# A longer first chunk and two buffers for the first attention pairs, in front of a TensorE-bound feed-forward layer

## The chip, the cores and the metric

The kernel runs on one core of one Trainium2 chip. The metric is the device time of one execution in microseconds (us). Five instruction streams run side by side on a core, each in the order in which it was built: TensorE (PE, matmuls; its weight loads are PEld), VectorE (DVE), ScalarE (ACT), GpSimd (POOL) and SyncE (SP), which here issues every DMA. SBUF is the working memory, PSUM the memory that TensorE writes.

## What is computed

Attention over 8 batches, 8 heads, 576 positions of 64 numbers, and behind it a feed-forward layer over the 4608 rows that come out of it:

```python
q_d, k_d, v_d = (a.reshape(B, H, 144, 4, D).mean(axis=3) for a in (q, k, v))
out_up = np.repeat(softmax(scale * q_d @ k_d.T) @ v_d, 4, axis=2)          # pooled
scores = np.where(abs(i - j) < 4, scale * q @ k.T, -1e9)                   # local band
x = out_up + softmax(scores) @ v                                            # (4608, 512)
h = x @ w_in                                                                # d_ff = 2048
g = np.where(h >= 1, h, np.where(h <= -1, 0.0, (h + 1) ** 2 / 4))
out = g @ w_out
```

(The softmax subtracts the row's maximum and divides by the sum plus 1e-9.)

## The kernel before

A **pair** is two heads of one batch; there are 32, four to a batch, written a0 to a31. For a pair, the 576 positions are covered by ten windows of 64, so local scores are twenty 64x64 products (`sl_ps`, L168), to which DVE adds a band mask (L186). DVE takes the row maximum, POOL subtracts it (L194), ACT takes the exponential (L197), DVE sums and divides. The pooled scores go the same way in three blocks of 48 queries (`sp_ps`, L178), for which ACT first writes q, scaled, into a block-diagonal tile `q_bd` (L153), so that one product serves both heads on 96 rows; ACT also divides them (L222). TensorE transposes both (`tl_ps` L234, `tp_ps` L243), ACT copies them out, TensorE multiplies with v (`pl_ps` L262, `pp_ps` L274), and DVE and ACT and POOL add them up and split x into a high and a low part, `xh` and `xl` (L283 to L295), in a ring of 1152 columns: two batches.

The feed-forward layer runs over 12 **chunks** of 384 columns, three to the ring, and 16 blocks f of 128 hidden units. A **step** is one (chunk, f): twelve matmuls into `h_ps` (`mm1`, L405), the activation on ACT, DVE and ACT (L416 to L421) giving `gh`, the rest `gl` on POOL (L422), and nine matmuls with 512 columns into three `o_ps` (`mm2`, L443). Chunk 0 needs batch 0 alone, chunk 1 and 2 also batch 1.

Weights arrive as raw 64-bit words, and each of 32 half-megabyte tiles is **converted** (`convert_weights`, "c" in the tables): two passes on ACT (L319, L322), two on DVE (L323, L324), a cast on ACT (L326), a subtraction on POOL (L327).

The order of the start is written out by hand in `BEFORE_STEPS` and `FIRST_STEPS`: q3 loads q and k of a3, v loads v of a0, w loads two weight tiles, c converts one, a5 goes on with a5 to its next yield, s is the next `mm1`, m the next `mm2`. A scheduler then orders each engine's stream, with `mm1`'s activation at a higher priority. Chunks 0 and 2 are split: both run first over f 0 to 7, then chunk 1 over all, then the other half of chunks 0 and 2; half sums of chunks 0 and 2 go through DRAM (`partial`). a8 to a11 are in the table; later pairs come from `attn_step`, one over four steps, in two chunks of three. When `FIRST_STEPS` ends, `mm2` is two steps behind `mm1`, and the loop that follows keeps it so.

One buffer each holds q, k, vp (v for pooling), v, qd, kd, sp, al, ap; PSUM tiles rotate for a0 to a3 over two (`rot1`) and three (`rot2`) buffers, and are single later.

Of the kernel before, what the change touches and what calls it, by code (L numbers as in the profile page):

```python
# [99 lines left out]
def attention_then_ffn(ctx: ExitStack, tc, qT, kT, vw, vp, band, w_in, w_out, out):  # L100
# [40 lines left out]

    def attention(n, pool_1, pool_2):
# [3 lines left out]
        M = 2 * QB  # L146


        qd = apool.tile([P, SD], F32, name="qd", tag="qd", bufs=1)
        nc.vector.tensor_reduce(qd, q.rearrange("p (s f) -> p s f", f=FACTOR), axis=AX.X, op=ALU.add)  # L150
        for h in range(2):
            hs = slice(h * D, (h + 1) * D)
# [5 lines left out]
        kd = apool.tile([P, SD], F32, name="kd", tag="kd", bufs=1)  # L158
# [367 lines left out]
```

## Time and profile before

| | |
|---|---|
| three runs | 1003.66, 1007.73, 1008.30 us (median 1007.73) |
| the profiled execution | 1004.22 us, of it 1002.4 us from first to last instruction (the span) |
| PE busy | 964.6 us (96%) |
| ACT, POOL, DVE busy | 534.6, 389.5, 364.1 us |
| mean granted TensorE clock | 0.985 of full speed |
| the chain that ended last | PE 85% of the span; `h_ps` 38%, `o_ps` 37% |
| DMA | 69.37 MB |

The chain is followed back from the last instruction; where it names one engine all along, that engine's own instructions add up to the time. Matmuls overlap, so a single one's duration is longer than the distance between two starts, and it is the distance that counts.

### The profile page before, as it was taken

The numbers are of one execution on the slowest core, as the hardware profiler recorded it, in microseconds if no ns is written. First come the engines' busy times: TensorE is split into PE (matmuls) and PEld (weight loads), VectorE is DVE, ScalarE is ACT, GpSimd is POOL, SyncE is SP. The second block draws the span as 40 slices with busy tenths as digits, with TensorE's granted clock in tenths as the row PEclk, the third lists the DMA queues.
The fourth block names the chain that finished last, engine by engine and source line by source line (L and its number), as shares of the span: only waits on it lengthen the run. The fifth ranks groups of instructions, "written<-read, shape, count | busy, mean of one in ns | idle before, by whom it ended". The sixth has DMA issues, their size and how long they took to land.

```text
span 1002.4 us, 18310 instructions
## 1 busy us (share of the span) xinstructions
PE 964.6 (96%) x7412; PEld 852.2 (85%) x7412; DVE 364.1 (36%) x646; ACT 534.6 (53%) x1221; POOL 389.5 (39%) x359
## 2 busy tenths in 40 slices
PE   5598999999999999999999999999999999999998
PEld 4477788899888888998888888999888888999997
DVE  5766464312445441113444343113334443111111
ACT  5768587544565555335555555434555555433433
POOL 3756664422345433223333344222344434222222
PEclk8699999999999999999999999999999999999999
DMA  7876210001324211002221222000212310000000
GB/s 261 297 263 229 79 52 33 0 1 56 113 75 137 74 50 57 1 1 80 63 62 50 81 61 62 32 1 26 80 52 73 97 58 14 33 1 1 32 1 31
DMA packets 28260, 69.37 MB, mean 69 GB/s; under 512 B 3344, under 2 KB 3344, under 8 KB 28176
## 3 DMA queue, kind: packets, MB, share of 16 engines
q1 hardware_dynamic: 28176, 68.20, 21.0%
q8 instruction: 58, 0.95, 0.4%
q14 instruction: 26, 0.21, 0.1%
...
## 4 chain that ended last, share of the span: by engine, by line
PE 85%; ACT 1%; DVE 1%; POOL 1%; issue 0%; DVEq 0%; ACTq 0%; POOLq 0%
PE h_ps L405 38%; PE o_ps L443 37%; PE sp_ps L178 2%; PE sl_ps L168 2%; PE pl_ps L262 2%; PE pp_ps L274 2%; PE tp_ps L243 1%; PE tl_ps L234 1%; POOL xl L295 0%; POOL sl L194 0%; POOL gl L422 0%; ACT u L417 0%; ACT u L416 0%; DVE sp_ps L212 0%; ACT gh L421 0%
## 5 line engine op out<-in xcount | busy, mean ns | idle before, releaser
L405 PE MATMUL h_ps<-xh,w_i 128*128 128x384 f32 x1536 | 404.3, 343 | 1.7 <-DVE u L418 1.4
L422 POOL TENSOR_TENSOR gl<-u,gh 128x384 fp32r<-128x384 f32 x192 | 195.4, 1018 | 505.6 <-ACT gh L421 391.0
L443 PE MATMUL o_ps<-w_o,gh 128*128 128x512 f32 x1152 | 358.0, 391 | 0.9 <-ACT osb L453 0.9
L405 PEld LDWEIGHTS h_ps<-xh,w_i 128*128 128x128 f32 x1536 | 276.5, 188 | 17.3 <-issue 4.8
L418 DVE SCALAR_TENSOR_TENSOR u<-h_ps,u 128x384 f32<-128x384 f32 x192 | 106.8, 556 | 449.2 <-ACT u L417 443.9
L405 PE MATMUL h_ps<-xl,w_i 128*128 128x384 f32 x768 | 261.2, 341 | 1.7 <-POOL xl L295 1.7
L443 PEld LDWEIGHTS o_ps<-w_o,gh 128*128 128x128 f32 x1152 | 213.7, 188 | 33.3 <-ACT osb L453 1.6
L443 PE MATMUL o_ps<-w_o,gl 128*128 128x512 f32 x576 | 226.0, 392 | 0.0
L416 ACT ACTIVATE u<-h_ps 128x384 f32<-128x384 f32 x192 | 94.3, 491 | 203.9 <-PE h_ps L405 201.0
L421 ACT CAST gh<-u 128x384 fp32r<-128x384 f32 x192 | 98.4, 513 | 95.9 <-DVE u L418 94.9
L405 PEld LDWEIGHTS h_ps<-xl,w_i 128*128 128x128 f32 x768 | 143.9, 188 | 3.0 <-POOL xl L295 2.7
L443 PEld LDWEIGHTS o_ps<-w_o,gl 128*128 128x128 f32 x576 | 108.3, 188 | 23.4 <-issue 0.6
L417 ACT ACTIVATE u<-u 128x384 f32<-128x384 f32 x192 | 100.0, 521 | 4.1
L208 ACT ACTIVATE sp<-sp_ps,mxp 96x144 f32<-96x144 f32 x96 | 36.1, 376 | 46.4 <-DVE mxp L206 44.0
L194 POOL TENSOR_TENSOR sl<-sl,mxl 128x640 f32<-128x640 f32 x32 | 41.7, 1303 | 44.7 <-DVE mxl L193 43.0
L295 POOL TENSOR_TENSOR xl<-x,xh 128x576 fp32r<-128x576 f32 x32 | 46.6, 1456 | 7.4 <-ACT xh L294 7.4
L226 POOL TENSOR_TENSOR vh<-vp_sb 72x512 f32<-72x512 f32 x32 | 42.0, 1312 | 17.0 <-DMA vp_sb<-vp 6.1
L285 DVE TENSOR_TENSOR x<-pl_ps,xd 128x576 f32<-128x576 f32 x32 | 24.2, 758 | 62.0 <-ACT xd L283 61.2
L212 DVE TENSOR_REDUCE sp_ps<-sl 128x10 f32<-128x640 f32 x32 | 26.5, 827 | 33.0 <-ACT sp L208 17.1
L222 ACT ACTIVATE sp<-sp,smp 96x144 f32<-96x144 f32 x96 | 34.8, 405 | 4.4 <-DVE smp L220 4.4
L234 PE MATMUL tl_ps<-ident,sl 128*128 128x128 f32 x160 | 23.9, 282 | 13.5 <-DVE sl L215 13.5
L186 DVE TENSOR_TENSOR sl<-sl_ps,band_sb 128x640 f32<-128x640 f32 x32 | 26.3, 823 | 28.2 <-PE sl_ps L168 28.2
...
## 6 DMA issues: line engine op xcount, KB each, us to landing
...
```

The source lines that it names most:

```text
L194: nc.gpsimd.tensor_tensor(slf, slf, ml.unsqueeze(2).broadcast_to([P, NB, WIN]), op=ALU.subtract)
L208: nc.scalar.activation(sp[:M, i], sp_v[:, i], AF.Exp, bias=mx[:M, i : i + 1], accum_out=psums[:, i : i + 1])
L222: nc.scalar.mul(sp[:M, i], sp[:M, i], sm[:M, i : i + 1])
L226: nc.gpsimd.tensor_tensor(vh, vpt[:, :, 0:2, :], vpt[:, :, 2:4, :], op=ALU.add)
L295: nc.gpsimd.tensor_tensor(xl[:, p, r0 : r0 + S], x, xh[:, p, r0 : r0 + S], op=ALU.subtract)
L405: nc.tensor.matmul(h[:, :TCH], wi[:, wt, cc * P : (cc + 1) * P], xt[:, cc, ts], start=(n == 0), stop=(n == 3 * NCC - 1),)
L416: nc.scalar.activation(u, h[:, :TCH], AF.Relu, bias=0.5, scale=0.5)
L417: nc.scalar.activation(u, u, AF.Square)
L418: nc.vector.scalar_tensor_tensor(u, h[:, :TCH], 1.0, u, op0=ALU.max, op1=ALU.min)
L421: nc.scalar.copy(gh, u)
L422: nc.gpsimd.tensor_tensor(gl, u, gh, op=ALU.subtract)
L443: nc.tensor.matmul(o, gt[:, ts], wo[:, wt, :], start=starts and n == 0, stop=ends and n == 2)
```

## The change

- `FIRST_STEPS` now takes chunk 0 through all 16 f, then the first four steps of chunk 1; the other chunks follow in order, nothing is split, and `partial` with its DMAs is gone. All 32 conversions and a4 to a7 stand in that stretch; a8 onward come from `attn_step`. `mm2` is one step behind `mm1` at its end.
- a1 and a3 get second buffers for kd, sp, vh/al, vd and ap/x, in SBUF that weight blocks 9 to 11 take later (`scratch`). For a0 to a3 the band is added by TensorE (two matmuls of the identity with the band, 384 and 256 columns, ahead of the twenty products, which then accumulate); DVE subtracts the maximum and POOL multiplies by the reciprocal of the sum, where it was the other way round.
- For all pairs: pooled scores are six products of 64 rows by 64 columns (each takes one quarter of the array, head h by half) instead of three of 128 by 96; `q_bd` and its ACT passes are gone, the scale sits in the exponential. The third block lies in the second bank of `sl_ps` with its heads swapped, and is issued second. The division of the pooled scores moves from three ACT passes to one DVE pass of 432 columns; the pooled transposes have 128 columns instead of 96.
- Conversions work in place in the raw tile, so they hold one shared temporary instead of two.

```diff
-HALF = NFC // 2
-SPLIT = (0, 2)
...
-    q0 a0 v a0 a0 q1 w q2 w a0 w a0 a0 a0 a1 a1 a1 a1 a0 c a0 c a1 a0 a1 a2 a2 q3 a1 a1
+    q0 v a0 a0 w q1 a0 a0 a1 w a1 q2 a0 a1 c a0 a1 a2 w c a0 a2 q3 a1 c a2 a0 a1 a2 a0 c
...
-    s s a4 c a5 a4 w a4 w w a5 a5 a4 s a6 a6 w a5 a6 a6 a6 a5 c c a5 a5 a6 m a5 c w s a6
...
+    a4 a4 w s a4 c c a4 w s a4 c c m a4 s w a4 m c c a4 a5 s w a5 a4 m a5 c c a5 a4 s w
...
+    second = {"kd": "wi9", "vd": "wo9", "sp": "wi10", "al": "wo10", "ap": "wi11"}
...
+    def scratch(n, shape, name, tag):
+        if n < NPAIR and n % 2:
+            return wpool.tile(shape, F32, name=f"{name}_{n}", tag=second[tag])
+        return apool.tile(shape, F32, name=name, tag=tag, bufs=1)
...
-            nc.scalar.mul(
-                q_bd[hs, :, h * QB : (h + 1) * QB],
-                qd[hs].rearrange("p (n s) -> p n s", n=NQB),
-                1.0 / (8.0 * FACTOR * FACTOR),
-            )
...
+        early = n < NPAIR
+        if early:
+            for c0, c1 in ((SL0, 512), (512, SL0 + NB * WIN)):
+                nc.tensor.matmul(
+                    sl_v[:, c0 - SL0 : c1 - SL0],
+                    ident_r,
+                    band_r.unsqueeze(1).broadcast_to([P, (c1 - c0) // WIN, WIN]),
+                    start=True,
+                    stop=False,
+                    skip_group_check=True,
+                )
...
-        sp_v = sp_ps[0:M, 0 : NQB * SD].rearrange("p (n s) -> p n s", n=NQB)
-        for i in range(NQB):
-            nc.tensor.matmul(sp_v[:, i, :], q_bd[:, i, :], kd, start=True, stop=True)
+        sp_v = sp_ps[:, 0 : 2 * SD].rearrange("p (n s) -> p n s", n=2)
+        sp_w = sl_ps[:, 1, 512 - SD :]
+        for i in (0, 2, 1):
+            for h in range(2):
+                hs = slice(h * D, (h + 1) * D)
+                nc.tensor.matmul(
+                    sp_v[hs, i, :] if i < 2 else sp_w[(1 - h) * D : (2 - h) * D, :],
+                    qd[hs, i * QB : i * QB + D],
+                    kd[hs, :],
+                    start=True,
+                    stop=True,
+                )
...
+        if early:
+            nc.vector.tensor_reduce(ml, sl_n, axis=AX.X, op=ALU.max)
+            nc.vector.tensor_tensor(slf, sl_n, ml_n, op=ALU.subtract)
+        else:
+            nc.vector.tensor_tensor(
+                slf, sl_n, band_sb.unsqueeze(1).broadcast_to([P, NB, WIN]), op=ALU.add
+            )
+            nc.vector.tensor_reduce(ml, slf, axis=AX.X, op=ALU.max)
+            nc.gpsimd.tensor_tensor(slf, slf, ml_n, op=ALU.subtract)
...
+        mx_ps = sp_ps[:, 2 * SD : 2 * SD + NQB]
+        sums = sp_ps[:, 2 * SD + 4 : 2 * SD + 4 + NB + NQB]
+        nc.vector.tensor_reduce(mx_ps[:, 2:3], sp_w, axis=AX.X, op=ALU.max)
+        nc.vector.tensor_reduce(mx_ps[:, 0:2], sp_v, axis=AX.X, op=ALU.max)
+        nc.vector.tensor_scalar_mul(mx, mx_ps, -scale)
+        for i in (2, 0, 1):
+            nc.scalar.activation(
+                sp[:, i],
+                sp_v[:, i] if i < 2 else sp_w,
+                AF.Exp,
+                bias=mx[:, i : i + 1],
+                scale=scale,
+                accum_out=sums[:, NB + i : NB + i + 1],
+            )
...
+        (nc.gpsimd if early else nc.vector).tensor_tensor(
+            slf, slf, parts[:, 0:NB].unsqueeze(2).broadcast_to([P, NB, WIN]), op=ALU.mult
+        )
...
+            sp, sp, parts[:, NB:].unsqueeze(2).broadcast_to([P, NQB, SD]), op=ALU.mult
...
-        for i in range(NQB):
-            nc.scalar.mul(sp[:M, i], sp[:M, i], sm[:M, i : i + 1])
...
+        high = t.bitcast(F32)[:, :, 1]
+        nc.scalar.activation(high, high, AF.Prelu, scale=2.0**-112, alpha=-(2.0**32))
+        nc.scalar.activation(t[:, :, 0], t.bitcast(U32)[:, :, 0], AF.Copy, scale=2.0**-29)
...
-        low = temp("low").bitcast(I32)
-        nc.scalar.activation(low, t.bitcast(U32)[:, :, 0], AF.Copy, scale=2.0**-29)
-        nc.vector.tensor_scalar(mi, mi, 3, None, op0=ALU.logical_shift_left)
-        nc.vector.tensor_tensor(mi, mi, low, op=ALU.add)
+        nc.vector.tensor_scalar(mi, t[:, :, 1], 3, None, op0=ALU.logical_shift_left)
+        nc.vector.tensor_tensor(mi, mi, t[:, :, 0], op=ALU.add)
...
-    later = {"n": 3 * NPAIR, "it": None, "pieces": None}
+    later = {"n": 2 * NPAIR, "it": None, "pieces": None}
...
-        starts = f == 0 or (c in SPLIT and f == HALF)
-        ends = f == NFC - 1 or (c in SPLIT and f == HALF - 1)
...
-    partial = dpool.tile([P, len(SPLIT), NTT, DM], F32, name="partial")
-    parts = [(0, 0, HALF), (2, 0, HALF), (1, 0, NFC), (0, HALF, NFC), (2, HALF, NFC)]
-    parts += [(c, 0, NFC) for c in range(3, NCH)]
-    steps = [(c, f) for c, f0, f1 in parts for f in range(f0, f1)]
+    steps = [(c, f) for c in range(NCH) for f in range(NFC)]
```

**The order of instructions.** Three places, as the two programs are built.

TensorE at the start of the program, before: L168 and L178 are local and pooled scores, L375 ten warm-up matmuls on the identity, L234 transposes.

```order
L168 MATMUL sl_ps<-first_o_87,first_i_86 64x64 x20
L178 MATMUL sp_ps<-kd,q_bd 96x144 x3
L375 MATMUL warm<-ident 128x128 x10
L178 MATMUL sp_ps<-kd,q_bd 96x144 x3
L234 MATMUL tl_ps<-ident,sl 128x128 x5
```

And now (L200 pooled scores, L417 the warm-up, L174 the band, L186 local scores):

```order
L200 MATMUL sp_ps<-kd,qd 64x144 x4
L417 MATMUL warm<-ident 128x128 x10
L174 MATMUL sl_ps<-band_r,ident_r 128x384
L174 MATMUL sl_ps<-band_r,ident_r 128x256
L186 MATMUL sl_ps<-first_o_89,first_i_88 64x64 x20
L200 MATMUL sl_ps<-kd,qd 64x144 x2
```

The warm-up stood behind the first pair's scores; now it stands between its pooled and its local scores.

TensorE in a stretch of later steps, before: w_i_1448 and w_i_1604 are w_in's blocks f = 8 and 9, w_o_1176 is w_out's block f = 6.

```order
L405 MATMUL h_ps<-xh,w_i_1448 128x384 x2
L405 MATMUL h_ps<-xl,w_i_1448 128x384
L443 MATMUL o_ps_4357<-w_o_1176,gh 128x512 x2
L443 MATMUL o_ps_4357<-w_o_1176,gl 128x512
L443 MATMUL o_ps_4358<-w_o_1176,gh 128x512 x2
L443 MATMUL o_ps_4358<-w_o_1176,gl 128x512
L443 MATMUL o_ps_4359<-w_o_1176,gh 128x512 x2
L443 MATMUL o_ps_4359<-w_o_1176,gl 128x512
L405 MATMUL h_ps<-xh,w_i_1604 128x384 x2
L405 MATMUL h_ps<-xl,w_i_1604 128x384
```

And now: w_i_842 and w_i_970 are blocks f = 5 and 6, w_o_773 is block f = 4.

```order
L447 MATMUL h_ps<-xh,w_i_842 128x384 x2
L447 MATMUL h_ps<-xl,w_i_842 128x384
L478 MATMUL o_ps_4235<-w_o_773,gh 128x512 x2
L478 MATMUL o_ps_4235<-w_o_773,gl 128x512
L478 MATMUL o_ps_4236<-w_o_773,gh 128x512 x2
L478 MATMUL o_ps_4236<-w_o_773,gl 128x512
L478 MATMUL o_ps_4237<-w_o_773,gh 128x512 x2
L478 MATMUL o_ps_4237<-w_o_773,gl 128x512
L447 MATMUL h_ps<-xh,w_i_970 128x384 x2
L447 MATMUL h_ps<-xl,w_i_970 128x384
```

Before, `mm2` of step 6 follows `mm1` of step 8; now `mm2` of step 4 follows `mm1` of step 5.

VectorE in a later pair, before, from one step's activation (L418) to the next: band, pooled maximum, local maximum, next pair's q, local sum.

```order
L418 SCALAR_TENSOR_TENSOR u<-h_ps,u 128x384
L186 TENSOR_TENSOR sl<-sl_ps,band_sb 128x640
L206 TENSOR_REDUCE mxp<-sp_ps 96x3
L193 TENSOR_REDUCE mxl<-sl 128x10
L150 TENSOR_REDUCE qd<-q_sb 128x144
L212 TENSOR_REDUCE sp_ps<-sl 128x10
L418 SCALAR_TENSOR_TENSOR u<-h_ps,u 128x384
```

And now (L460 is the activation, L236 to L238 the pooled maximum, L161 the next pair's q):

```order
L460 SCALAR_TENSOR_TENSOR u<-h_ps,u 128x384
L221 TENSOR_TENSOR sl<-sl_ps,band_sb 128x640
L236 TENSOR_REDUCE sp_ps<-sl_ps 128x1
L224 TENSOR_REDUCE mxl<-sl 128x10
L237 TENSOR_REDUCE sp_ps<-sp_ps 128x2
L161 TENSOR_REDUCE qd<-q_sb 128x144
L238 TENSOR_SCALAR mxp<-sp_ps 128x3
L460 SCALAR_TENSOR_TENSOR u<-h_ps,u 128x384
```

The pooled maximum comes in three instructions, and its last one, which the pooled exponentials wait for, has moved behind the reduction of the next pair's q.

## Rows read from the trace of the kernel before

**Rows 1.** The chain of waits in order of time: start, duration, what. First two pieces 21.18 us apart in a stretch with pairs, then two in a stretch without, then the end.

```profile
342.36 2.29 PE h_ps L405 x12
...
363.54 2.29 PE h_ps L405 x12
...
907.31 2.12 PE h_ps L405 x12
...
911.47 2.12 PE h_ps L405 x12
...
992.63 6.13 PE o_ps L443 x27
```

**Rows 2.** Busy time of PE by stretch (from:to, length, busy with its count, granted clock, DMA share, GB/s), of three lines alone: `mm1` (L405), then `mm2` (L443), then the pooled product that ends a pair's work on PE (L274, 8 to a pair).

```profile
0.00:140.00 140.00, 34.12 (x161) 0.89 0.63 211
...
0.00:200.00 200.00, 65.03 (x324) 0.92 0.45 152
...
0.00:140.00 140.00, 28.12 (x99) 0.89 0.63 211
...
0.00:200.00 200.00, 59.77 (x231) 0.92 0.45 152
...
0.00:140.00 140.00, 6.21 (x64) 0.89 0.63 211
```

**Rows 3.** Busy time by stretch of all engines: from:to, length, PE, PEld, DVE, ACT, POOL (each with its count), granted clock, DMA share, GB/s. The fourth has two pairs and eight steps, the last ten steps and no pair.

```profile
0.00:58.20 58.20, 33.50 (x486) 28.41 (x486) 37.57 (x69) 37.29 (x95) 30.73 (x32) 0.77 0.79 273
...
58.20:100.00 41.80, 37.58 (x346) 31.41 (x344) 28.82 (x53) 33.32 (x83) 26.66 (x23) 0.96 0.74 250
...
100.00:140.00 40.00, 36.61 (x339) 29.92 (x338) 20.90 (x34) 26.65 (x61) 23.74 (x20) 1.00 0.27 82
...
321.18:363.54 42.36, 42.36 (x380) 37.13 (x379) 17.71 (x32) 23.39 (x56) 17.43 (x18) 1.00 0.19 59
...
890.00:931.60 41.60, 41.60 (x211) 38.10 (x211) 5.58 (x11) 15.28 (x30) 10.10 (x10) 1.00 0.00 1
```

**Rows 4.** Timeline of the start, PE and then POOL: start, duration, engine, line, operation, output and inputs, count, idle time before and what ended it. L234 at 18.26 is the first pair, at 53.27 the fourth; L405 is the first step; POOL's row is the fourth pair's `xl`.

```profile
9.45 3.75 PE L375 MATMUL warm<-ident 128*128 128x128 f32 x20
...
18.26 0.76 PE L234 MATMUL tl_ps<-ident,sl 128*128 128x128 f32 x5 [4.33 <-DVE sl L215]
...
53.27 0.71 PE L234 MATMUL tl_ps<-ident,sl 128*128 128x128 f32 x5
...
58.23 0.62 PE L405 MATMUL h_ps<-xh,w_i 128*128 128x384 f32 x2
...
60.28 1.45 POOL L295 TENSOR_TENSOR xl<-x,xh 128x576 fp32r<-128x576 f32 x1 [0.91 <-ACT xh L294]
```

**Rows 5.** Groups by line: line, engine, operation, tiles, shapes, count, busy us, mean ns of one, idle before.

```profile
L319 ACT ACTIVATE m<-raw_i 128x512 f32<-128x512 f32 x16 | 10.6, 666 | 2.0 <-POOL w_i L327 1.2 <-POOL gl L422 0.6
...
L326 ACT CAST w_i<-m 128x512 fp32r<-128x512 f32 x16 | 9.8, 614 | 1.8 <-DVE m L324 1.7
...
L324 DVE CUSTOM_DVE_ANT_0 m<-m,low 128x1024 uint16<-128x1024 uint16 x32 | 30.2, 943 | 7.5 <-ACT low L322 6.4
...
L323 DVE TENSOR_SCALAR m<-m 128x512 int32<-128x512 int32 x32 | 18.1, 566 | 17.9 <-ACT m L319 17.9
...
L327 POOL TENSOR_TENSOR w_i<-m,w_i 128x512 fp32r<-128x512 f32 x16 | 21.7, 1357 | 20.2 <-ACT w_i L326 20.2
...
L222 ACT ACTIVATE sp<-sp,smp 96x144 f32<-96x144 f32 x96 | 34.8, 405 | 4.4 <-DVE smp L220 4.4
...
L153 ACT ACTIVATE q_bd<-qd 64x144 f32<-64x144 f32 x64 | 20.3, 317 | 3.2 <-DVE qd L150 2.7
...
L206 DVE TENSOR_REDUCE mxp<-sp_ps 96x3 f32<-96x432 f32 x32 | 19.3, 602 | 5.1 <-PE sp_ps L178 3.6
...
L215 DVE TENSOR_TENSOR sl<-sl,sp_ps 128x640 f32<-128x640 f32 x32 | 26.2, 819 | 0.9
...
L208 ACT ACTIVATE sp<-sp_ps,mxp 96x144 f32<-96x144 f32 x96 | 36.1, 376 | 46.4 <-DVE mxp L206 44.0 <-PE tp_ps L243 0.8
```

**Rows 6.** Timeline of PE in a later pair: local scores, pooled scores, the step behind them; then the pooled transposes and what follows them.

```profile
325.48 0.92 PE L168 MATMUL sl_ps<-k_sb,q_sb 64*64 64x64 f32 x40
...
326.33 0.98 PE L178 MATMUL sp_ps<-kd,q_bd 128*96 128x144 f32 x6
...
327.05 0.62 PE L405 MATMUL h_ps<-xh,w_i 128*128 128x384 f32 x2
...
336.99 0.69 PE L243 MATMUL tp_ps<-ident,sp 96*72 96x96 f32 x6
...
337.46 0.42 PE L405 MATMUL h_ps<-xl,w_i 128*128 128x384 f32 x1
```

**Rows 7.** Timeline of one step without a pair: the last matmul of `mm1`, the first pass of its activation, `gl`.

```profile
863.32 0.34 PE L405 MATMUL h_ps<-xl,w_i 128*128 128x384 f32 x1
...
863.69 0.49 ACT L416 ACTIVATE u<-h_ps 128x384 f32<-128x384 f32 x1 [1.86 <-PE h_ps L405]
...
866.08 1.02 POOL L422 TENSOR_TENSOR gl<-u,gh 128x384 fp32r<-128x384 f32 x1 [3.16 <-ACT gh L421]
```

**Rows 8.** Timeline of the later pair of rows 6: SP issues the next pair's q, DVE reduces it.

```profile
326.44 0.34 SPq L130 DMA_DIRECT2D q_sb<-qT  x1
...
329.79 0.75 DVE L150 TENSOR_REDUCE qd<-q_sb 128x144 f32<-128x576 f32 x1 [1.11 <-DMA q_sb<-qT]
```

More of the change, by code (lines that the diff above doesn't have):

```diff
@@ L113, in attention_then_ffn @@
     nc.sync.dma_start(band_sb, band)
-    q_bd = cpool.tile([P, NQB, 2 * QB], F32, name="q_bd")
-    nc.gpsimd.memset(q_bd, 0.0)
+    ident_r = cpool.tile([P, P], F32R, name="ident_r")
+    nc.scalar.copy(ident_r, ident)
+    band_r = cpool.tile([P, WIN], F32R, name="band_r")
+    nc.scalar.copy(band_r, band_sb)
+    qd = cpool.tile([P, NQB * QB + D - QB], F32, name="qd")
+    nc.gpsimd.memset(qd[:, SD:], 0.0)
     xh = cpool.tile([P, NCC, RING], F32R, name="xh")
@@ L145, in attention @@
         q, k = qk[p] if b == 0 else (loaded["q"], loaded["k"])
[L146 to L152, printed above, removed]
[L153 to L158 removed]
+        copy = nc.scalar.copy
+        nc.vector.tensor_reduce(
+            qd[:, 0:SD], q.rearrange("p (s f) -> p s f", f=FACTOR), axis=AX.X, op=ALU.add
+        )
+        kd = scratch(n, [P, SD], "kd", "kd")
         nc.vector.tensor_reduce(kd, k.rearrange("p (s f) -> p s f", f=FACTOR), axis=AX.X, op=ALU.add)
@@ L197, in attention @@
         nc.scalar.activation(slf, slf, AF.Exp, scale=0.125)
         yield
-        sp = apool.tile([P, NQB, SD], F32, name="sp", tag="sp", bufs=1)
+        sp = scratch(n, [P, NQB, SD], "sp", "sp")
+        scale = 1.0 / (8.0 * FACTOR * FACTOR)
         mx = small(NQB, "mxp")
-        sm = small(NQB, "smp")
-        sums = sp_ps[:, NQB * SD : NQB * SD + NB]
-        psums = sp_ps[:M, NQB * SD + NB : NQB * SD + NB + NQB]
-        nc.vector.tensor_reduce(mx[:M], sp_v, axis=AX.X, op=ALU.max, negate=True)
@@ L210, in attention @@
             )
         yield
-        nc.vector.tensor_reduce(sums, slf, axis=AX.X, op=ALU.add)
+        nc.vector.tensor_reduce(sums[:, 0:NB], slf, axis=AX.X, op=ALU.add)
         nc.vector.tensor_scalar_add(sums, sums, 1e-9)
-        nc.vector.reciprocal(sums, sums)
-        nc.vector.tensor_tensor(
-            slf, slf, sums.unsqueeze(2).broadcast_to([P, NB, WIN]), op=ALU.mult
+        parts = small(NB + NQB, "sums") if early else sums
+        nc.vector.reciprocal(parts, sums)
+        (nc.gpsimd if early else nc.vector).tensor_tensor(
+            slf, slf, parts[:, 0:NB].unsqueeze(2).broadcast_to([P, NB, WIN]), op=ALU.mult
@@ L217, in attention @@
         )
         yield
-        nc.vector.tensor_scalar_add(psums, psums, 1e-9)
-        nc.vector.reciprocal(sm[:M], psums)
-        for i in range(NQB):
-            nc.scalar.mul(sp[:M, i], sp[:M, i], sm[:M, i : i + 1])
-        vh = apool.tile([KB, NKB, 2, P], F32, name="vh", tag="al", bufs=1)
+        nc.vector.tensor_tensor(
+            sp, sp, parts[:, NB:].unsqueeze(2).broadcast_to([P, NQB, SD]), op=ALU.mult
+        )
+        vh = scratch(n, [KB, NKB, 2, P], "vh", "al")
         vpt = loaded["vp"]
@@ L432, in mm2 @@
             ]
-        if c in SPLIT and f == NFC - 1:
-            sums = []
-            for t in range(NTT):
-                sums.append(temp("first"))
-                nc.sync.dma_start(sums[t], partial[:, c // 2, t, :])
         wo = weights["o", f]
```

83 lines of the change are left out of this document (33 added, 50 removed).

## Prediction

> **What bounds the kernel now.** I read the page first, then the chain of waits, then the stretches of the start, then single instructions. The chain is TensorE alone: in stretches without pairs its pieces repeat every 4.16 us (911.47 - 907.31), twelve matmuls of `mm1` in 2.12 us and nine of `mm2` in 2.04; with a pair in four steps they repeat every 21.18 us, so a pair costs TensorE 21.18 - 4 x 4.16 = 4.54 us [rows 1]. All the work at this rate is 192 x 4.16 + 32 x 4.54 = 944 us of a span of 1002.4. The other 58.4 us are what can be won; the reader is to see where they lie. By 200 us, 324 matmuls of `mm1` (0.177 us each), 231 of `mm2` (0.227) and eight pairs are done: 57.3 + 52.4 + 36.3 = 146 us of work, 54 lost. By 140 us it is 28.5 + 22.5 + 36.3 = 87.3, 52.7 lost [rows 2]. So the whole loss lies at the start, but for some 4 us at the end (the last `mm2` ends at 998.76). At 58.23 us, when the first `mm1` begins [rows 4], four pairs and the fifth one's scores are done (4 x 4.54 + 1.6 = 19.8): 38.4 us are lost by then, in a stretch in which the granted clock is 0.77 and no engine is full, DVE and ACT being busy 37.6 and 37.3 of 58.2 us [rows 3]. From there to 140 us TensorE does 67.5 us of work in 81.8, a rate of 0.825.
>
> **The start up to the first step.** The engines' work there hardly changes: an early pair saves three ACT divisions and two passes for `q_bd` (3 x 0.405 + 2 x 0.317 = 1.85 us) and moves 0.82 us of multiplication from DVE to POOL, where a subtraction of like size leaves; DVE gains a pass of 432 columns (0.60, after the maximum of 432 columns) [rows 5]. What changes is the overlap. The transposes of the first and fourth pair stand at 18.26 and 53.27 [rows 4], 11.7 us per pair. With two buffers the closest spacing is DVE's work: a pair is (17.71 - 8 x 0.51) / 2 = 6.8 us on it, 0.51 a step being from the stretch without pairs [rows 3]; plus 0.6, less 0.8, is 6.6, and four conversions of 1.51 us lie in the stretch by the new order: (3 x 6.6 + 6.0) / 3 = 8.6 us per pair. Bounds are 8.6 and 11.7 (nothing won, since qd, q's maximum, vp and v still have what they had); I take 8.6, since ACT's share of the same stretch, three pairs of 4.4 us, ten conversion passes of 0.67 and four casts of 0.61, is 7.5 a pair. That is 9.2 us earlier. Against it stands the warm-up, which now runs between the first pair's pooled and local scores: up to 3.7 us [rows 4], taken in full. The band's matmuls (640 columns, 0.25 us at 0.39 ns a column, 0.5 at half clock) lie in TensorE's idle time. From the fourth pair's transposes to the end of its `xl`, 8.5 us, I leave as it is: 61.7 becomes 56.2. By then TensorE has done four pairs, the fifth's scores and one `mm1`, 21.7 us: 34.5 lost.
>
> The weights' DMAs go to SP in a new order, the tiles of f = 3 and on behind v of later pairs. By 52 us some 13 MB must have come, 252 GB/s; the trace has 273 in that stretch [rows 3]. I cost it at nothing; if a tile comes late, ACT's passes over it hold up the pair's casts behind them.
>
> **Chunk 0 through all weights.** Up to its last `mm1` TensorE has 15 x 2.12 + 14 x 2.04 + 8 x 4.37 - 21.7 = 73.7 us of work (4.37 is below). ACT's order puts 28 of its 64 conversion passes and 6 of 32 casts ahead of the fourth pair's x; it has in this stretch 36 passes of 0.67, 25 casts of 0.61, four pairs of 4.4 and 14 steps of 1.35: 76 us (a step is 15.28 us less three output copies, each as long as a cast, over ten; a pair is (23.39 - 8 x 1.35) / 2 = 6.3, less 1.85). DVE has 26 conversions of 1.51, four pairs of 7.4 and 14 steps of 0.51: 75. POOL has 26 x 1.36 + 4 x 4.7 + 14 x 1.0 = 68 [rows 3, 5]. Before, the same engines had 60, 50 and 50 us in 81.8, because half of the conversions came later, under a full TensorE. So four engines are nearly alike, each waits for the others in a fixed order, and none can fill another's gap. I take the rate that the trace has, 0.825: 89.3 us, 15.6 lost; bounds are 0.93 (80 us, ACT at 95%) and 0.75 (98 us). The start then loses 34.5 + 15.6 = 50.1 instead of 54: **-3.9 us**. The removed DMAs of half sums and their copies cost TensorE under 1 us before; I count nothing. Strided conversions in place aren't in the trace; 0.1 us more a pass would be 6 us of ACT, inside the lower bound.
>
> **Later pairs.** Pooled scores took 327.05 - 326.33 = 0.72 us for six passes. Now there are twelve of 64 by 64 with 144 columns. The nearest row is that of the local scores, 40 passes of 64 columns in 0.85 us, 21 ns each [rows 6]. By columns this is 48 ns, 0.57 us in all; by columns and loaded weights together (208 to 128) 35 ns, 0.41. I take 0.50, 0.22 less. Transposes with 128 columns for 96: six in 0.47 us now [rows 6], a third more columns is at most 0.08; I take 0.05 more. So -0.17 a pair (-0.26 to -0.02), 24 pairs: **-4.1 us** (-6.3 to -0.5).
>
> What speaks against this term: the two heads' products use different row halves but write one bank. A column costs (227 - 177) / 128 = 0.39 ns, so 64 columns alone take 25 ns and 144 take 56. If the halves took turns, twelve passes would take 0.67 us and next to nothing would be won. The local scores' 21 ns, in the same arrangement, is only a little less than 25, so overlap is shown, but not much of it.
>
> The Trainium skill has that as a rule: TensorEngine Tiling (Array Packing), Gotcha 1 (PSUM Pressure), says that different row tiles can't access the same PSUM bank simultaneously. By that rule the pooled scores win nothing and the sum rises by 4.1; the trace's 21 ns agrees with it in part at most.
>
> **`mm2` one step behind.** After `mm1` ends, `gh` is ready 2.4 us later and `gl` 3.45 (863.66, 866.08, 867.10) [rows 7]. Two steps behind, TensorE has three products more of other steps to do, about 8.3 us; one step behind, 4.16, and `gl` is wanted 0.45 after that. Without a pair 1.1 us of slack are left. In the last step there is only one `mm2` in between: 0.3 for `gh` and 0.65 for `gl`, **+1.0 us**. With a pair, DVE now does the pooled maximum's last instruction behind the next pair's qd, which waits for a DMA issued only after the local scores: issue at 0.96 us after their start, qd at 4.31 to 5.06 [rows 8]. Then 0.2 for the small instruction; on ACT two pooled exponentials of about 0.5 (0.38 and a read of the sum) stand ahead of the cast to `gh`: 6.3, cast 6.8, `gl` 7.9 with POOL's 1.0. TensorE wants it at 1.45 + 2.12 + 2.04 + 2.12 + 0.45 = 8.2. So 0.3 us are left; some q will come later. I take 0.05 a pair, **+1.2 us** (0 to 14).
>
> **Sum.** -3.9 - 4.1 + 1.0 + 1.2 = -5.8. The profiled execution took 1004.22 us (1.8 outside the span), so 998.4, forecast **998**; the median of the three runs, 1007.73, is 0.35% above that execution, and I don't correct for it.
>
> **Rivals.**
> - Chunk 0 flows better: conversions hold one shared temporary less (ACT's first pass waited 1.2 us for POOL's last [rows 5]) and TensorE reaches 0.93: 9.3 us less, **989**. Against it: ACT would be 95% busy, which no 40 us of the start show.
> - The change doesn't do what it says: with qd, vp, v and q's maximum as they were, pairs follow each other as now, or four full engines give 0.75. Either costs 9 us: **1007**. For it: the equal loads above.
> - Slower: `gl` comes late in each later pair. It decides when q lands over 0.3 us later than in rows 8; each 0.1 us beyond is 2.4 us over 24 pairs. 0.6 us late: +14, **1012**. For it: TensorE's cover is halved; against it: q has its usual 3.3 us.
> - Row halves take turns in a bank, 0.67 us for the pooled scores and 0.05 more for the transposes: no term for later pairs, **1002**.
>
> **How the numbers follow.** Forecast 0.40, flows better 0.20, start no better 0.20, `gl` late 0.12, banks 0.08. Under 0.5%, about 5 us, a measurement of this kernel can't tell from no change: faster is below 999.2, slower above 1009.2. Faster: 0.26 of the forecast's 0.40 (its own range is 992 to 1005), 0.20, and 0.02 of the rest: 0.48. Slower: 0.10 of the late `gl`, 0.07 of the start: 0.19, with 0.02 for what I haven't seen. The range 985 to 1012 takes in the bounds of start and pairs and leaves out the ends of the second and third rival.
>
> **What would show it.** The first `mm1`'s last matmul at 56 us, against 61 to 63; pooled transposes 8 to 9 us apart in the first four pairs; chunk 0's last `mm1` at about 145; a pair's period in later chunks 21.0 us with pooled scores at 0.5. Wrong would be: TensorE idle before `mm2` with `gl` as releaser in each pair, a period over 21.2, or a first step at 60 or later.

## The result, and the profile after

The changed kernel takes 1012.08 us (median of five, 1010.77 to 1012.96) against 1007.73 (1003.66 to 1009.04): 1.0052 times the time before, with a 95% interval of 1.0028 to 1.0077. It is slower by half a per cent; 998 was forecast, with a range up to 1012. The profiled execution took 1010.77 us with a span of 1009.0 (before 1004.22 and 1002.4), so 6.6 us are to be found.

First the counts that answer to [rows 2]: busy time by stretch, PE and then PEld, for `mm1` (L447 now), `mm2` (L478) and the pooled product (L318) alone.

```profile
0.00:200.00 200.00, 63.80 (x312) 55.82 (x312) 0.92 0.43 145
...
0.00:200.00 200.00, 57.39 (x220) 41.06 (x221) 0.92 0.43 145
...
0.00:200.00 200.00, 6.21 (x64) 3.96 (x64) 0.92 0.43 145
```

By 200 us that is 312 x 0.177 + 220 x 0.227 + 8 x 4.45 = 140.8 us of work (a pair now costs 21.09 - 4 x 4.16 = 4.45 us), so 59 are lost, where before lost 54 and the forecast was 50. By then 12 products of `mm1` and 11 of `mm2` fewer are done than before, 12 x 0.177 + 11 x 0.227 = 4.6 us: so much of the 6.6 us arises in the start and chunk 0. Here is how far the start got, to be held against [rows 4]: transposes of the first and fourth pair, the first step, the fourth pair's `xl`.

```profile
23.46 1.33 PE L272 MATMUL tl_ps<-ident,sl 128*128 128x128 f32 x5 [3.50 <-POOL sl L254]
...
49.64 1.33 PE L272 MATMUL tl_ps<-ident,sl 128*128 128x128 f32 x5 [1.82 <-POOL sl L254]
...
55.22 0.62 PE L447 MATMUL h_ps<-xh,w_i 128*128 128x384 f32 x2
...
56.99 1.44 POOL L337 TENSOR_TENSOR xl<-x,xh 128x576 fp32r<-128x576 f32 x1 [3.16 <-ACT xh L336]
```

The pairs do follow each other faster, (49.64 - 23.46) / 3 = 8.7 us for 11.7. But the first one's transposes come 5.2 us later than the 18.26 of before, and its wait is for GpSimd's division. The stretches of all engines, as in [rows 3] (PE, PEld, DVE, ACT, POOL, clock, DMA, GB/s):

```profile
0.00:58.20 58.20, 36.09 (x535) 28.25 (x535) 36.94 (x63) 37.01 (x81) 30.10 (x31) 0.82 0.74 242
58.20:100.00 41.80, 36.13 (x260) 28.61 (x258) 40.34 (x59) 33.37 (x72) 32.00 (x25) 0.96 0.72 264
100.00:140.00 40.00, 35.10 (x324) 28.96 (x325) 32.37 (x49) 28.39 (x64) 25.65 (x22) 0.91 0.20 62
```

From 58.2 to 100 us DVE is busy 40.3 of 41.8 us, where it had 28.8. At the same time TensorE does less than before: 36.1 us after 37.6. In the third stretch its granted clock is 0.91, where [rows 3] have 1.00: it stood at the lower of its two levels (1.2 for 2.4 GHz) from 108.5 to 112.0 and from 122.2 to 125.6 us, after stretches in which TensorE was busy 7.2 of 10.5 and 8.3 of 10.2 us. That takes at most 0.09 x 40 = 3.6 us, an estimate from the two rows that takes TensorE as busy all the time. What fills DVE are the conversions. Their groups, as in [rows 5] (shift L365, add L366):

```profile
L366 DVE CUSTOM_DVE_ANT_0 m<-raw_o,m 128x1024 uint16<-128x1024 uint16 x16 | 19.5, 1216 | 0.8 <-ACT raw_o L362 0.8
...
L366 DVE CUSTOM_DVE_ANT_0 m<-raw_i,m 128x1024 uint16<-128x1024 uint16 x16 | 16.6, 1040 | 0.2 <-ACT raw_i L362 0.2
L365 DVE TENSOR_SCALAR m<-raw_i 128x512 int32<-128x512 int32 x16 | 15.5, 967 | 4.0 <-ACT raw_i L360 3.1 <-POOL gl L464 0.9
L365 DVE TENSOR_SCALAR m<-raw_o 128x512 int32<-128x512 int32 x16 | 14.4, 901 | 0.0
```

The same 32 shifts and adds take 66.0 us, 2.06 for a shift and its add, where [rows 5] have 48.3, 1.51 each. 26 of the 32 lie between 58.2 and 160 us, and take 55.5 us there, 2.13 each (the same groups in that window):

```profile
L366 DVE CUSTOM_DVE_ANT_0 m<-raw_o,m 128x1024 uint16<-128x1024 uint16 x13 | 16.2, 1245 | 0.0
L365 DVE TENSOR_SCALAR m<-raw_i 128x512 int32<-128x512 int32 x13 | 14.2, 1093 | 0.9 <-POOL gl L464 0.9
L366 DVE CUSTOM_DVE_ANT_0 m<-raw_i,m 128x1024 uint16<-128x1024 uint16 x13 | 14.2, 1090 | 0.0
L365 DVE TENSOR_SCALAR m<-raw_o 128x512 int32<-128x512 int32 x13 | 10.9, 839 | 0.0
```

It isn't their new strides: the shortest shift is 0.41 us in both kernels. DVE and POOL side by side at 66 to 75 us show what it is (start, duration, line):

```profile
66.67 1.22 DVE L365 TENSOR_SCALAR m<-raw_o 128x512 int32<-128x512 int32 x1
...
68.14 1.78 DVE L366 CUSTOM_DVE_ANT_0 m<-raw_o,m 128x1024 uint16<-128x1024 uint16 x1
...
71.12 1.37 DVE L366 CUSTOM_DVE_ANT_0 m<-raw_i,m 128x1024 uint16<-128x1024 uint16 x1
...
72.56 1.07 DVE L365 TENSOR_SCALAR m<-raw_o 128x512 int32<-128x512 int32 x1
73.56 0.81 DVE L254 TENSOR_TENSOR sl<-sl,sp_ps 128x640 f32<-128x640 f32 x1
...
66.15 1.45 POOL L464 TENSOR_TENSOR gl<-u,gh 128x384 fp32r<-128x384 f32 x1
68.05 1.33 POOL L369 TENSOR_TENSOR w_i<-m,w_i 128x512 fp32r<-128x512 f32 x1 [0.44 <-ACT w_i L368]
...
71.90 1.45 POOL L464 TENSOR_TENSOR gl<-u,gh 128x384 fp32r<-128x384 f32 x1
73.32 1.46 POOL L369 TENSOR_TENSOR w_i<-m,w_i 128x512 fp32r<-128x512 f32 x1
```

The shift at 66.67 ends at 67.89, 0.29 us after GpSimd's subtraction (66.15 + 1.45 = 67.60). The add at 68.14 ends 0.54 after GpSimd's next (69.38), the shift at 72.56 0.28 after the one that ends at 73.35. Each spends its time waiting for GpSimd's instruction to end, and then does its work. The multiplication at 73.56 (L254), whose second operand is in PSUM, takes its usual 0.81 us right beside GpSimd. It goes the other way too: the `gl` of 71.90 begins while the add of 71.12 runs (to 72.49), and takes 1.45 us where the median is 1.01. Where GpSimd's instructions follow each other, one instruction of VectorE can wait through more than one of them:

```profile
38.46 2.67 DVE L365 TENSOR_SCALAR m<-raw_o 128x512 int32<-128x512 int32 x1
...
37.77 1.69 POOL L369 TENSOR_TENSOR w_i<-m,w_i 128x512 fp32r<-128x512 f32 x1
39.41 1.43 POOL L337 TENSOR_TENSOR xl<-x,xh 128x576 fp32r<-128x576 f32 x1
```

This shift ends at 41.13, 0.29 us after the second of the two (40.84). It holds for the whole trace: 35 of the 64 shifts and adds take over 0.05 us longer than the shortest (0.41 and 0.67 us), 31 us in all, and each of them ends 0.28 to 0.29 us (shifts) or 0.55 (adds) after the end of a GpSimd instruction. Before, it was 18 of 64, and 13 us.

The Trainium skill says this as a rule (SBUF — State Buffer, Who interferes with whom): VectorE and GpSimd share a pair of SBUF ports, a VectorE instruction needs it in a two-port mode, or with both inputs in SBUF beside a GpSimd instruction that reads SBUF, and whichever comes second waits for the whole of the other's instruction. The rows above agree with that line by line; the shift of 38.46 waited for two.

After 200 us there is a gain and a loss. The rows that answer to [rows 6], pooled scores with the step behind them, and the pooled transposes:

```profile
290.04 0.86 PE L186 MATMUL sl_ps<-k_sb,q_sb 64*64 64x64 f32 x38
290.68 0.34 PE L200 MATMUL sl_ps<-kd,qd 64*64 64x144 f32 x2
290.73 0.23 PE L186 MATMUL sl_ps<-k_sb,q_sb 64*64 64x64 f32 x2
290.78 0.29 PE L200 MATMUL sp_ps<-kd,qd 64*64 64x144 f32 x2
290.85 0.29 PE L200 MATMUL sl_ps<-kd,qd 64*64 64x144 f32 x2
290.91 0.54 PE L200 MATMUL sp_ps<-kd,qd 64*64 64x144 f32 x6
291.37 0.62 PE L447 MATMUL h_ps<-xh,w_i 128*128 128x384 f32 x2
...
301.30 0.85 PE L284 MATMUL tp_ps<-ident,sp 128*72 128x128 f32 x6
301.90 0.42 PE L447 MATMUL h_ps<-xl,w_i 128*128 128x384 f32 x1
```

Local and pooled scores take 1.33 us for 1.57, the transposes 0.60 for 0.47: 0.11 won a pair, and the period is 21.09 us for 21.18. The eight passes into `sp_ps` start in four couples, 0.01 us apart in a couple and 0.12 from one couple to the next (290.78, 290.91, 291.03, 291.15). Two passes of one product began 0.12 apart before, so a couple must be one pass of each head; the four passes of the third block (`sl_ps`) run beside them. But where a chunk ends, it is longer, and the last step shows two waits:

```profile
306.12 0.71 PE L318 MATMUL pp_ps<-ap,vd 72*64 72x144 f32 x8
...
327.57 0.71 PE L318 MATMUL pp_ps<-ap,vd 72*64 72x144 f32 x8
...
1001.63 0.73 PE L478 MATMUL o_ps<-w_o,gh 128*128 128x512 f32 x2 [0.35 <-ACT gh L463]
1002.71 0.50 PE L478 MATMUL o_ps<-w_o,gl 128*128 128x512 f32 x1 [0.35 <-POOL gl L464]
```

327.57 - 306.12 is 21.45 us, 0.36 more than inside a chunk, and 0.7 us are waited for `gh` and `gl` at the end. The 0.36 are lost in front of a pair's local transposes, which wait for VectorE's division (the row counts 0.17 of it as idle time; the product before them has its next start due at 321.77, 0.33 earlier):

```profile
322.10 0.74 PE L272 MATMUL tl_ps<-ident,sl 128*128 128x128 f32 x5 [0.17 <-DVE sl L254]
```

The trace has such a wait at six chunk ends (at 237, 322, 474, 558, 710 and 794 us), where a pair runs across the end; at the others there is none.

### The profile page after: what moved, and what is told of

Its sections match the earlier page's. It is cut to its first block, busy times and chain, and to the rows that moved or that the text cites. A ratio compares the mean times of both kernels' runs of the same rounds, so it can differ in the third digit from the quotient of the medians.

```text
span 1009.0 us, 18511 instructions
## 1 busy us (share of the span) xinstructions
PE 967.4 (96%) x7612; PEld 845.8 (84%) x7612; DVE 386.9 (38%) x668; ACT 488.3 (48%) x1063; POOL 391.1 (39%) x359
## 4 chain that ended last, share of the span: by engine, by line
PE 79%; DVE 6%; issue 6%; POOL 3%; ACT 3%; DMA 2%; SPq 0%; POOLq 0%; DVEq 0%; ACTq 0%
PE h_ps L447 35%; PE o_ps L478 33%; PE tp_ps L284 2%; PE sl_ps L186 2%; PE pl_ps L306 2%; PE tl_ps L272 2%; DVE m L366 2%; PE pp_ps L318 2%; POOL gl L464 2%; DVE m L365 1%; PE sp_ps L200 1%; DMA first_o<-kT 1%; DMA raw_i<-w_in 1%; POOL sl L225 1%; ACT sp L240 0%
## 5 line engine op out<-in xcount | busy, mean ns | idle before, releaser
L447 PE MATMUL h_ps<-xh,w_i 128*128 128x384 f32 x1536 | 405.7, 344 | 0.0
L478 PE MATMUL o_ps<-w_o,gh 128*128 128x512 f32 x1152 | 358.2, 392 | 0.4 <-ACT gh L463 0.4
L447 PEld LDWEIGHTS h_ps<-xh,w_i 128*128 128x128 f32 x1536 | 277.0, 188 | 20.8 <-issue 10.9
L460 DVE SCALAR_TENSOR_TENSOR u<-h_ps,u 128x384 f32<-128x384 f32 x192 | 106.8, 556 | 453.4 <-ACT u L459 425.4
L447 PE MATMUL h_ps<-xl,w_i 128*128 128x384 f32 x768 | 262.4, 342 | 0.0
L478 PEld LDWEIGHTS o_ps<-w_o,gh 128*128 128x128 f32 x1152 | 214.2, 188 | 32.6 <-ACT gh L463 1.2
L478 PE MATMUL o_ps<-w_o,gl 128*128 128x512 f32 x576 | 226.2, 393 | 4.3 <-POOL gl L464 4.3
L447 PEld LDWEIGHTS h_ps<-xl,w_i 128*128 128x128 f32 x768 | 144.6, 188 | 0.7 <-POOL xl L337 0.3
L478 PEld LDWEIGHTS o_ps<-w_o,gl 128*128 128x128 f32 x576 | 108.4, 188 | 30.0 <-POOL gl L464 7.1
L225 POOL TENSOR_TENSOR sl<-sl,mxl 128x640 f32<-128x640 f32 x28 | 35.5, 1267 | 43.8 <-DVE mxl L224 43.8
L221 DVE TENSOR_TENSOR sl<-sl_ps,band_sb 128x640 f32<-128x640 f32 x28 | 23.1, 824 | 41.6 <-PE sl_ps L200 41.6
L306 PEld LDWEIGHTS pl_ps<-al,v_sb 64*64 64x64 f32 x1280 | 23.9, 144 | 15.7 <-issue 8.8
L284 PE MATMUL tp_ps<-ident,sp 128*72 128x128 f32 x192 | 29.5, 293 | 4.5 <-ACT sp L240 2.5
```

The lines of the kernel that those rows point to most:

```text
L225: nc.gpsimd.tensor_tensor(slf, slf, ml_n, op=ALU.subtract)
L284: nc.tensor.transpose(tp_v[:, kb, i, :], sp[:, i, kb * KB : (kb + 1) * KB], ident if i < 2 else swapped,)
L306: nc.tensor.matmul(pl_v[hs, o : o + OUT_LEN[i]], v[rs, 2 * g + h, :], al[rs, g, c0 : c0 + OUT_LEN[i]], start=True, stop=True,)
L447: nc.tensor.matmul(h[:, :TCH], wi[:, wt, cc * P : (cc + 1) * P], xt[:, cc, ts], start=(n == 0), stop=(n == 3 * NCC - 1),)
L460: nc.vector.scalar_tensor_tensor(u, h[:, :TCH], 1.0, u, op0=ALU.max, op1=ALU.min)
L478: nc.tensor.matmul(o, gt[:, ts], wo[:, wt, :], start=f == 0 and n == 0, stop=f == NFC - 1 and n == 2)
```

## The experiments

The theory after this reading (**port**): chunk 0 through all weights puts the conversions' shifts and adds on DVE beside GpSimd's subtractions, and what the two wait for each other inside their instructions is the loss. The rivals: **lag** (`mm2` waits, since it is only one step behind `mm1`), **exchange** (the first pairs' band on TensorE and their division on GpSimd), **warm-up**, and **order** as a whole. Ratios are to the kernel before, with 95% intervals; where none stands, times are medians.

**The lag.** The first of these drops the first `m` of FIRST_STEPS, so that all of chunk 0 has a lag of two; the second drops the last.

```diff
-    a4 a4 w s a4 c c a4 w s a4 c c m a4 s w a4 m c c a4 a5 s w a5 a4 m a5 c c a5 a4 s w
+    a4 a4 w s a4 c c a4 w s a4 c c a4 s w a4 m c c a4 a5 s w a5 a4 m a5 c c a5 a4 s w
```

```diff
-    m s m s m s m s m
+    m s m s m s m s
```

> Every mm2 two steps behind its mm1 again, chunk 0 included. If the one-step lag is what costs (gl waited for in chunk 0, 3.9 us on TensorE, and 1.4 at the end): 1006 to 1008 us. If VectorE, held up by GpSimd, is the limit of chunk 0: only the end comes back, 1010.5.

> mm2 two steps behind only from the end of the table on. Both theories: the end's 1.4 us come back, 1010.5; the difference to the run with the lag everywhere is what the lag costs in chunk 0 (4 us or more by the one, under 1 by the other).

The late lag alone gives 1008.90 us (1.0015, 1.0002 to 1.0028), 3.2 less than the change. Its pairs have the same period (21.10), also across a chunk's end (302.47 to 323.58), so the 0.36 at each of six chunk ends and the 0.7 at the end, 2.9 us, are what it saves. With the lag of two everywhere the time is 1012.02 (1.0058, 1.0040 to 1.0077): what the end wins, chunk 0 loses. So the rival falls for chunk 0, where one step behind is the better by some 3 us, and holds behind it.

**The port.** GpSimd's part taken out, then VectorE's, then GpSimd's part moved to VectorE (all of it, and w_in's half):

```diff
-        nc.gpsimd.tensor_tensor(w[:, 1], m, w[:, 0], op=ALU.subtract)
+        nc.gpsimd.tensor_tensor(w[:, 1, 0:16], m[:, 0:16], w[:, 0, 0:16], op=ALU.subtract)
...
-                    wi[:, wt, cc * P : (cc + 1) * P],
+                    wi[:, 0, cc * P : (cc + 1) * P],
...
```

(`mm2` likewise reads `wo[:, 0, :]` for `wo[:, wt, :]`.)

> GpSimd's subtraction of a conversion cut to 16 columns (the low parts of the weights are left out, and the products that use them take the high part): 32 times 1.4 us less on GpSimd. If VectorE's shift and add are long because GpSimd holds them up: they fall to 0.42 and 0.69 us everywhere, VectorE's 40.3 of 41.8 us in 58:100 to under 33, and the time to 1006 or less. If they are long by themselves: busy times stay, and the time with them (over 1010).

997.34 us (0.9908, 0.9889 to 0.9926), 14.7 less than the change. The shifts and adds fall from 66.0 us to 49.5 (20.5 + 29.0), and by 160 us 46 us are lost instead of 59, counted as above. They don't fall to the 0.42 and 0.69 us that were expected, but to 1.55 for both together, since GpSimd's other instructions are still there. DVE stays busy in 58:100 (38.0 us, not under 33), but with more done, and TensorE gains 2.1 us there and 1.6 in the next stretch, at a granted clock of 1.00 in both for 0.96 and 0.91 (columns as above):

```profile
58.20:100.00 41.80, 38.27 (x322) 31.37 (x320) 38.00 (x68) 38.69 (x84) 20.75 (x27) 1.00 0.73 270
100.00:140.00 40.00, 36.67 (x353) 30.79 (x354) 30.83 (x49) 28.89 (x65) 23.45 (x29) 1.00 0.20 63
```

```diff
+        m = temp("m")
+        nc.scalar.activation(m, high, AF.Prelu, scale=2.0**-112, alpha=-(2.0**32))
-        nc.scalar.activation(high, high, AF.Prelu, scale=2.0**-112, alpha=-(2.0**32))
...
-        m = temp("m")
-        nc.vector.tensor_scalar(mi, t[:, :, 1], 3, None, op0=ALU.logical_shift_left)
-        nc.vector.tensor_tensor(mi, mi, t[:, :, 0], op=ALU.add)
+        nc.vector.tensor_scalar(mi[:, 0:16], mi[:, 0:16], 3, None, op0=ALU.logical_shift_left)
+        nc.vector.tensor_tensor(mi[:, 0:16], mi[:, 0:16], t[:, 0:16, 0], op=ALU.add)
```

> VectorE's shift and add of a conversion cut to 16 columns (the low bits of the weights are left out), GpSimd's subtraction whole again. If VectorE, held up by GpSimd, is the limit of chunk 0: 66 us less on it, and as much won as without the subtraction, 998 to 1000 us. If GpSimd's own queue is the limit, because gl comes late behind the subtractions: under 5 us won, 1007 or more.

995.74 us (0.9889, 0.9870 to 0.9907), 16.3 less than the change: as much as from GpSimd's side, so it isn't GpSimd's queue alone. This run also shows the port by itself. The shift has 16 columns here, and the second line gives its shortest, median and longest time in ns; below it the GpSimd instruction beside one of them.

```profile
L365 DVE TENSOR_SCALAR m<-m x32: 158/176/2714, 10.6 to 137.7; 128x16 int32<-128x16 int32 x32
```

```profile
70.21 1.23 DVE L365 TENSOR_SCALAR m<-m 128x16 int32<-128x16 int32 x1 [1.46 <-ACT m L361]
...
70.14 1.27 POOL L369 TENSOR_TENSOR w_i<-m,w_i 128x512 fp32r<-128x512 f32 x1
```

A shift of 0.16 us takes 1.23: it ends at 71.44, GpSimd's subtraction at 71.41.

The 14.7 and 16.3 are not the price of the port alone. Both runs take away work together with the waits, up to 45 us of GpSimd's or 35 of VectorE's (32 x 1.08, at the shortest). In both the granted clock is 1.00 from 58.2 to 140 us; against the change's 0.96 and 0.91 that is worth at most 0.04 x 41.8 + 0.09 x 40 = 5.3 us, an estimate from the rows. No run parts work, waits and clock from each other; the next two leave nothing out.

```diff
-        nc.gpsimd.tensor_tensor(w[:, 1], m, w[:, 0], op=ALU.subtract)
+        nc.vector.tensor_tensor(w[:, 1], m, w[:, 0], op=ALU.subtract)
```

> With the late lag of two, the subtraction of every conversion on VectorE, so that nothing is left out: 45 us less on GpSimd, 32 times about 0.7 us more on VectorE, less what it no longer waits for GpSimd. GpSimd's queue the limit: 996 to 1000 us. VectorE the limit: what it takes on (22 us) eats what it saves (14 to 18), 1005 to 1012.

> The same for w_in's conversions alone, w_out's stay on GpSimd. Halfway between the run with the late lag (1008.9) and the run with all of them on VectorE, unless the two engines are the limit at different times; then below both.

Both have the late lag of two. 1003.24 us (0.9965, 0.9950 to 0.9980) and 1003.68 (0.9973, 0.9959 to 0.9987), for the 1008.90 of their base: 5.7 and 5.2 won with nothing left out, but VectorE is full then (41.2 of 41.8 us in 58:100 with all of them). Whether the kernel before pays the same for its port:

> The kernel before with GpSimd's subtraction cut to 16 columns (low parts of the weights left out, as in the run of the changed kernel, which won 14.8 us). If the loss on VectorE and GpSimd is made by squeezing all conversions into chunk 0: much less won here, 5 to 9 us. If both kernels pay it alike: 13 to 15 us, 992 to 994, and something else makes the changed kernel slower.

1002.43 us (0.9951, 0.9931 to 0.9970): 5.0 won, a third of the 14.7. The theory says why: 12 of before's 32 conversions begin after 140 us, and from there to 200 us TensorE is busy 59.1 of 60 us all the same. Part of the contrast is the clock again: in this run it is 0.90 in 58:100, for 0.96 before.

**The warm-up and the order.** `WARM = 1` in place of 10; and the steps, split halves and lag of before with the new attention. The new attention holds the local scores' PSUM place until the pooled exponentials are done, so some twenty entries of the old tables had to move, all of the fifth pair and later.

> One warm-up product in place of ten. If the 3.7 us between pair 0's pooled and local scores delay the start: first mm1 3 us earlier and 1009 us. If the chain over VectorE and GpSimd sets the first four pairs: no change, or worse by a lower clock, 1011 to 1014.

> The order, the split halves and the lag of before with the new attention and conversions. If the order through all weights loses the time: the kernel before less the later pairs' gain, 1005 to 1006. If the new attention or the conversions in place lose it: 1010 or more.

With one warm-up product 1008.44 (1.0019, 1.0007 to 1.0032), 3.6 won, with the first `mm1` at 51.91 for 55.22. The old order took 1024.87 (1.0180, 1.0161 to 1.0198) with 46 us lost by 58.2, where the kernel before, counted alike, has 40. So its first four pairs, whose entries didn't move, are already late: the old order doesn't suit the new attention, and the run says nothing on the question it was to answer. The order as a rival of its own stays untested.

**The exchange, and a surprise.**

```diff
-        early = n < NPAIR
+        early = False
```

> The first four pairs with the band on VectorE, the subtraction on GpSimd and the division on VectorE, as in later pairs; second buffers and order as changed. If the exchange shortens the spacing of these pairs: 4 us lost, 1016. If its GpSimd division gives back what the band saves: 1010 to 1013.

1003.48 us (0.9968, 0.9955 to 0.9981), 8.6 less than the change, though the first transposes at 19.34 and the first `mm1` at 53.07 explain only 2 to 4. The rest is in the plain steps. The starts of an `mm1`, its `mm2` and what follows, first of the changed kernel, then of this run:

```profile
295.64 0.52 PE L447 MATMUL h_ps<-xh,w_i 128*128 128x384 f32 x2
...
297.76 0.62 PE L478 MATMUL o_ps<-w_o,gh 128*128 128x512 f32 x2
```

```profile
333.01 0.51 PE L447 MATMUL h_ps<-xh,w_i 128*128 128x384 f32 x2
...
335.09 0.62 PE L478 MATMUL o_ps<-w_o,gh 128*128 128x512 f32 x2
```

`mm1` takes 2.08 us instead of 2.12, and a step 4.133 instead of 4.160 to the end of the kernel: 0.027 x 192 = 5.2 us. Nothing in a step is changed. But without the exchange the two small buffers `sums` aren't made, and the weights, `gh` and `gl` lie 128 bytes lower in SBUF (`xh` and `xl` don't move). Two runs to part the causes:

```diff
+        if n < NPAIR:
+            nc.vector.memset(small(NB + NQB, "sums"), 0.0)
-        parts = small(NB + NQB, "sums") if early else sums
+        parts = sums
```

> The exchange undone, but the small buffer sums still made (and set to zero), so that all buffers lie where they do in the changed kernel. If placement makes the steps shorter: 4.16 us a step and 1008.5, 3 us won by the start alone. If the exchange does it: 4.133 and 1003.5, as without the buffer.

```diff
-        parts = small(NB + NQB, "sums") if early else sums
+        parts = wpool.tile([P, NB + NQB], F32, name=f"sums_{n}", tag="wo11") if early else sums
```

> The changed kernel with sums in a weights' buffer that is still free, so that the weights, gh and gl lie 128 bytes lower. If placement makes the steps shorter: 4.133 us a step and 1006.5 to 1007.5. If the exchange does it: 4.16 and 1012.

The exchange undone with the old place: 4.160 us a step and 1007.94 (1.0005, 0.9991 to 1.0019). The exchange kept with the other place: 4.133 and 1006.32 (0.9997, 0.9984 to 1.0010). So the place is worth 4.5 to 5.8 us and the exchange costs 2.8 to 4.1. The kernel before, moved by 128 bytes:

```diff
+    pad = apool.tile([P, 32], F32, name="pad", tag="pad", bufs=1)
+    nc.vector.memset(pad, 0.0)
```

> The kernel before with an idle buffer of 128 bytes in front of its attention buffers, so that weights, gh and gl lie 128 bytes higher. If the step time goes by the place and 128 bytes are what turns it: 4.133 us a step and 1002 us. If it only concerns the places of the changed kernel: 4.16 and 1007.4.

4.133 us a step, 1002.23 (0.9949, 0.9930 to 0.9968). Both kernels as given have the slow place, so it is no part of their difference.

**Together.** The three that won alone; the same mends on the kernel before; the exchange undone with the late lag, then with the low parts on VectorE, and with one warm-up product.

> The changed kernel with the three things that won alone: lag of two from the table's end on, the low parts on VectorE, one warm-up product. If the three are separate losses: 1003.2 less 3.7, 999.5 us. If the start that is won goes to the same waits in chunk 0: 1002 to 1003.

> The kernel before with the low parts on VectorE and one warm-up product, nothing left out. If the order of before leaves VectorE room: 1000 to 1003 us, as good as the changed kernel so mended. If the low parts there stand in the way of its steps: 1005 or more.

> The exchange undone and the late lag of two together. If their gains add: 1003.5 less 3.2, 1000.3 us.

> The same with the low parts of the weights on VectorE. If the three add: 1000.3 less 5.7, 994.6 us. If VectorE, which has the band and the division of four pairs back, is full in the start: 998 or more.

> The exchange undone, the late lag of two, one warm-up product. If the warm-up delays the start here too: 999.1 less 3, 996. If it only did so because the band's product stood behind it on TensorE: 999 or more.

Late lag, low parts on VectorE and one warm-up product: 1004.18 (0.9969, 0.9957 to 0.9982), no better than without touching the warm-up (1003.24). In the profiled executions the first transposes come 0.8 us earlier than there (21.6 for 22.4), but the first `mm1` comes 1.0 later, at 55.63 for 54.62: what the start wins is gone again before chunk 0. The kernel before with low parts on VectorE and one warm-up product: 1007.69 (1.0007, 0.9995 to 1.0019), nothing won. **The exchange undone and the late lag: 999.08 (0.9920, 0.9905 to 0.9934)**, the fastest with the whole computation, 0.8% under before. With the low parts on VectorE it is 1002.64 (0.9954, 0.9939 to 0.9968), with one warm-up product 1002.48 (0.9958, 0.9940 to 0.9976): the mends of the start don't add. The fastest run still pays for the port: its shifts and adds take 65.7 us, and taking the subtractions off GpSimd, which won 5.7 us on the change with the late lag, costs 3.6 here.

## Why the prediction was wrong

- **Start up to the first step.** The spacing was right: 8.7 us for a forecast 8.6. The first pair is 5.2 us late for 3.7, and the fourth pair's `xl` ends at 58.4 for 56.2. What I had not priced was the exchange itself: I let 0.82 us move from DVE to POOL at no cost, and undoing it wins 2.8 to 4.1 us. The runs don't part what of that is the band's product standing behind the warm-up, what is GpSimd's division, for which TensorE waits 3.5 us once, and what is the pooled division, which now takes its factors from SBUF (`sums`) and needs 0.61 to 2.13 us where 0.59 to 0.60 is usual. A step on DVE was misread, too: [rows 3] give 5.58 us for ten steps, 0.56 and not 0.51, which changes the spacing by 0.2 us.
- **Chunk 0: the step that failed.** I priced 26 conversions at 1.51 us on DVE, the mean of before, and took the new load as if engines only queue for their own work. In 58.2 to 160 us the 26 took 55.5 us, 2.13 each: 16 us more. The mean of before already held waits for GpSimd (1.51 against 0.41 + 0.66 at the shortest; 13 of the 48.3 us), and a price that holds waits isn't fixed: it grows with how much of both engines runs at once, which was what this change raised: 31 us of waits for 13. So 22 us were lost from the first step to 200 us where I had 15.6. How much of these 6 us goes through the waits and how much through the lower clock isn't parted by any run. That two engines share one resource was in none of my rivals; "four full engines give 0.75" was the nearest, argued from equal loads and not from this.
- **Later pairs.** Right in kind, half in size: 0.09 us a pair for 0.17. The scores won 0.24 where I had 0.22; the transposes cost 0.13 where I had 0.05 and called 0.08 the most (a third of their 0.47 is 0.16). 24 pairs give 2.2 us for 4.1. The row halves did not take turns in the bank: the twelve pooled passes take 0.48 us (1.33 less the 0.85 of the local scores in [rows 6]), near my 0.50. But the ways to both were wrong. A pass of 144 columns took 0.12 us before (0.72 / 6), 0.83 ns a column; the 0.39 are those of `mm1` and `mm2`. Taking turns would have cost twelve times 0.12, 1.4 us, and not 0.67, and what the trace shows is the passes of both heads side by side, each at the 0.12 of before. So the rule cited in the prediction does not show here, and that 0.50 was met is luck.
- **`mm2` one step behind.** 3.2 us for 2.2, but not where I put it. The end cost 0.7 (1.0 forecast), inside a chunk a pair costs nothing (1.2 forecast), and 0.36 us come at six chunk ends. There the trace has ACT's three output copies between the pooled exponentials, VectorE's sum waits for the last exponential, and the transposes wait for the division behind it; that the copies are the cause wasn't tried alone. The late `gl` of every pair did not happen. In chunk 0 the short lag even helps.
- **Sum.** With the exchange undone and the long lag behind the table the change is worth something: 999.08, where the kernel before takes 1002.23 at a place as fast. That is 3.2 us less, where 8 (the 5.8 and the 2.2 of the lag) were forecast; 1.9 of the missing 4.8 us are those of the later pairs.

What stays open: why a lag of two costs 3 us in chunk 0, what the new order is worth by itself, and what the port costs alone. That VectorE's conversions are lengthened by GpSimd is shown, instruction by instruction; that this is what chunk 0 lost is argued from runs that took away work and changed the clock as well.
